# k and q issued ahead of the centroids, other idle products on TensorE, and one placed copy cut in two

## The chip, the core and the metric

The kernel runs on one core of a Trainium2 chip. The core has a matrix engine (TensorE, PE in the profile), a vector engine (VectorE, DVE), an activation engine (ScalarE, ACT), a general engine (GpSimd, POOL) and SyncE (SP), which here only issues DMAs. The engines run their own instruction streams in order and wait for one another through semaphores. The metric is the device time of the program in microseconds, the median of several runs; lower is better.

## What is computed

The reference is clustered attention over 2 batches of 8 heads, sequence 768, head size 64, followed by two dense feed-forward layers. A query sees a key only if both have the same nearest centroid:

```
q_assign = argmax(einsum("bhsd,hcd->bhsc", q_n, c_n)); k_assign likewise     # c_n: centroids / norm
scores = where(q_assign == k_assign, (q @ k.T) / 8, -1e9)
x = softmax(scores) @ v                                                     # then (1536, 512)
h = x @ moe_w_in;  x = max(0.01 * h, h) @ moe_w_out
h = x @ moe2_w_in; out = max(h, 0)**2 @ moe2_w_out
```

## The kernel before

Heads are worked on in pairs (two heads fill 128 partitions); there are eight pairs. Each operand of the score products is held as a high and a low part, which are placed into a tile `hb` of one head (rows 0 to 63 and 64 to 127, four slots of 768 columns). For the first pair the parts are computed straight into `hb` by VectorE, ScalarE and GpSimd; for later pairs they are computed into a tile `spl` and copied into `hb` by DMAs that SP issues (`place`, L482, letters a to d are the four copies of a head; c is the low part of q, into rows 64 to 127 of slot 0). A unit of attention is two tiles of 128 queries: score products S0 and S1 (L521), row maxima R0 and R1 (L543), exponentials X0 and X1 (L553), row sums RE and RC, the scaling N0 and N1 (L570), transposes Ta to Tc (L583), their copies Ha to Hc and La to Lc (L594, L600) and the products with v, Va to Vc (L618). Tile t writes its scores into PSUM bank set t % 2.

The order on all engines in this part of the program is written by hand. The string `RAMP` (L51) lists the operations of the first pair and the start of the second one by one; every engine takes its own operations in that order. After it a repeating table takes over, then the two feed-forward layers with orders of their own.

Ahead of `RAMP` stand the constants and the loads. SP issues the centroids `ct` (L326), then k and q of pair 0 and of pair 1 (`loads_qk`, L323, tile `rqk`), then v. `prep_centroids` (L333) computes the norm of each centroid: a product and a sum on VectorE (L335, L337), a square root on ScalarE (L339), and on VectorE a lower bound, a reciprocal, one correction step, another reciprocal and the scaling of `ct` (L341 to L351). TensorE transposes `ct` into `ctp` (L353), and ScalarE copies that into `cbd` (L355, L356), a block-diagonal tile which GpSimd has set to zero (L170). Products of k and q with `cbd` are the dots (L391) from which VectorE chooses the clusters (L782, L785). ScalarE needs a function table for the square root and another for the exponential, so it runs two table loads. While TensorE has nothing to do it runs idle products of an identity matrix (`warm_up`, L328, nine ahead of `ctp` and three behind it, and `fill`, L772), whose results nobody reads. A float32 product of this kind appears as two records.

`head_0` (L705) makes the parts of head 0: on VectorE four operations (L714, L721, L714, L725) that follow the centroid work in its order, on ScalarE two (L712) that follow the copies of `cbd`.

Of the kernel before, what the change touches and what calls it, by code (L numbers as in the profile page):

```python
# [8 lines left out]
F32 = mybir.dt.float32  # L9
# [5 lines left out]
AF = mybir.ActivationFunctionType  # L15
ALU = mybir.AluOpType
# [87 lines left out]
def attention_moe_moe_kernel(  # L104
# [9 lines left out]
    nc = tc.nc  # L114
    NP, _, _, S = qk.shape
# [9 lines left out]
    HALF = S // 2  # L125
# [24 lines left out]
    const = ast.enter_context(tc.tile_pool(name="const", bufs=1))  # L150
    const.tile([128, 120], F32, name="cpad")

    ident = const.tile([128, 128], F32, name="ident")
    make_identity(nc, ident)
    eps = const.tile([128, 1], F32, name="eps")
    nc.gpsimd.memset(eps, 1e-9)
    msc = const.tile([128, 1], F32, name="msc")
    mbi = const.tile([128, 1], F32, name="mbi")
    nc.gpsimd.memset(msc[0:32], BIG)
# [7 lines left out]
    identb = const.tile([128, 128], BF16, name="identb")  # L167
    nc.gpsimd.tensor_copy(out=identb, in_=ident)
    cbd = const.tile([128, HP, 2 * C], F32, name="cbd")
    nc.gpsimd.memset(cbd, 0.0)  # L170
    desc = const.tile([128, 24, C], F32, name="desc")
    for c in range(C):
        nc.gpsimd.memset(desc[:, :, c], float(2 ** (C + 8 - c)))
# [149 lines left out]
            nc.sync.dma_start(out=rqks[p][:, j], in_=qk[p, j])  # L323

    ct = const.tile([128, D], F32, name="ct")
    nc.sync.dma_start(out=ct, in_=cen)  # L326

    def warm_up(n):  # L328
        w = ps_t.tile([128, 512], F32, tag="T", name="warm")
        for i in range(n):  # L330
            nc.tensor.matmul(out=w[:, 0:128], lhsT=ident, rhs=ident, start=True, stop=True)  # L331

    def prep_centroids():  # L333
        sq = const.tile([128, D], F32, name="sq")
        nc.vector.tensor_tensor(out=sq, in0=ct, in1=ct, op=ALU.mult)  # L335
        ss = const.tile([128, 1], F32, name="ss")
        nc.vector.tensor_reduce(out=ss, in_=sq, axis=AX.X, op=ALU.add)  # L337
        n0 = const.tile([128, 1], F32, name="n0")
        nc.scalar.activation(out=n0, in_=ss, func=AF.Sqrt)  # L339
        nc.scalar.activation(out=const.tile([128, 1], F32, name="tab"), in_=eps, func=AF.Exp)  # L340
        nc.vector.tensor_scalar(out=n0, in0=n0, scalar1=1e-30, scalar2=None, op0=ALU.max)  # L341
        rn = const.tile([128, 1], F32, name="rn")
        nc.vector.reciprocal(out=rn, in_=n0)
        nc.vector.scalar_tensor_tensor(
            out=n0, in0=ss, scalar=rn, in1=n0, op0=ALU.mult, op1=ALU.add
        )
        nc.vector.tensor_scalar(
            out=n0, in0=n0, scalar1=0.5, scalar2=1e-6, op0=ALU.mult, op1=ALU.add
        )
        nc.vector.reciprocal(out=rn, in_=n0)  # L350
        nc.vector.tensor_scalar(out=ct, in0=ct, scalar1=rn, scalar2=None, op0=ALU.mult)  # L351
        ctp = ps_t.tile([128, 512], F32, tag="T", name="ctp")
        nc.tensor.transpose(ctp[0:64, 0:128], ct, ident)  # L353
        cview = ctp[0:64, 0:128].rearrange("p (a h c) -> p a h c", h=2, c=C)
        nc.scalar.copy(out=cbd[0:64, :, 0:C], in_=cview[:, :, 0])  # L355
        nc.scalar.copy(out=cbd[64:128, :, C : 2 * C], in_=cview[:, :, 1])  # L356
# [125 lines left out]
    def place(p, j, which):  # L482

        h = 2 * p + j
        r = slice(64 * j, 64 * j + 64)
        if h not in hbs:
            hbs[h] = heads[h % 3]
        hb = hbs[h].bitcast(F32)
        sp = spl[p].bitcast(F32)
        copies = {  # L490
            "a": (hb[0:64, 0:3], sp[r, 0:3]), "b": (hb[0:64, 3], sp[r, 0]),
            "c": (hb[64:128, 0], sp[r, 3]), "d": (hb[64:128, 1], sp[r, 1]),
        }
        for c in which:
            o, i = copies[c]
            nc.sync.dma_start(out=o, in_=i)
# [196 lines left out]
    for h, j in ((2, 3), (0, 2), (0, 3), (1, 2), (1, 3)):  # L693
        nc.sync.dma_start(
            out=heads[h][80:128, j].bitcast(F32), in_=heads[2][80:128, 2].bitcast(F32)
        )
    warm_up(9)
    prep_centroids()
    eighth = const.tile([128, 1], F32, name="eighth")
    warm_up(3)  # L700

    for h in range(2):
        hbs[h] = heads[h]
# [90 lines left out]
    def mask_mm(h, part, cols=(0, 1, 2)):  # L794
        j, g = 1 - part // 2, part % 2
        mt = mask_t[h, part, cols] = ps_t.tile([128, 512], F32, tag="T", name="ohT")
        for i in cols:
            o = (2 * (g * (KC // 2) + i) + h) * C
            nc.tensor.transpose(
                mt[0:80, i * 128 : (i + 1) * 128], flat[:, 1 - j, o : o + 80], ident  # L800
            )

    def mask_act(h, part, cols=(0, 1, 2), act=None):
        j, g = 1 - part // 2, part % 2
        c = slice(cols[0] * 128, (cols[-1] + 1) * 128)
        mt = mask_t.pop((h, part, cols))[64:80, c]
        o = hbs[h][64:80, 3 - j, g * HALF + c.start : g * HALF + c.stop]
        act = j == 1 if act is None else act
        if j == 1:
            (nc.scalar.copy if act else nc.vector.tensor_copy)(out=o, in_=mt)  # L810
        elif act:
            nc.scalar.activation(
                out=o, in_=mt, func=AF.Identity, bias=mbi[64:80], scale=msc[64:80]
            )
        else:
            nc.vector.tensor_scalar(
                out=o, in0=mt, scalar1=msc[64:80], scalar2=mbi[64:80], op0=ALU.mult, op1=ALU.add
            )
# [20 lines left out]
    for h in range(2):  # L839
        for i in range(4):  # L840
            if (h, i) != (0, 2):
                first_ops[f"mk{h}{i}"] = lambda h=h, i=i: mask_mm(h, i)
                first_ops[f"ma{h}{i}"] = lambda h=h, i=i: mask_act(h, i)
                first_ops[f"ma{h}{i}A"] = lambda h=h, i=i: mask_act(h, i, act=True)
                first_ops[f"ma{h}{i}D"] = lambda h=h, i=i: mask_act(h, i, act=False)
        first_ops[f"ms{h}"] = lambda h=h: place_masks(1, h, (2, 3, 0, 1))
        for c in "abcd":
            first_ops[f"pl{h}{c}"] = lambda h=h, c=c: place(1, h, c)
    first_ops.update(head_1())

# [14 lines left out]
    for g, c in enumerate("abc"):  # L865
# [28 lines left out]
        "oT": oh_trans,  # L894
        "st": mask_rows,
        "pl00": lambda p: place(p, 0, "abcd"),
        "pl01": lambda p: place_masks(p, 0),
        "pl10": lambda p: place(p, 1, "abcd"),
# [11 lines left out]
    for op in RAMP.split():  # L910
        if ":" in op:
            name, i = op.split(":")
            step(name, int(i), unit_ops[name])
        elif "@" in op:
            name, i = op.split("@")
# [6 lines left out]
    for u in range(-1, NU + 5):  # L922
# [9 lines left out]
        for op in PLAN[u % UPP].split():  # L932
            if ":" in op:
                name, lag = op.split(":")
                i = u - int(lag)
                if 0 <= i < NU:
                    step(name, i, unit_ops[name])
            else:
                name, ahead = op.split("@")
# [6 lines left out]
        w = u - (NU - UPP)  # L946
# [610 lines left out]
```

## Time and profile before

| What | us |
|---|---|
| median of 3 runs | 733.88 (733.5 to 734.03) |
| the profiled execution, own time | 734.87 |
| its span, first to last instruction | 733.1 |
| PE / POOL / DVE / ACT busy | 725.6 / 596.5 / 562.3 / 500.0 |

The profiled execution's own time is 1.77 us above its span: what lies around the instructions. It is also 0.99 us above the median of the runs. A row of the trace in order of time reads: start, duration, engine, line, operation, what it writes and reads, size, count, and in brackets how long the engine had been idle and what is taken to have ended that. Where that last part names an engine that had long been done, it was something else that came last, often a DMA.

### The profile page before, as it was taken

Reading aid. Unit: us, or ns where it says so; the run is one execution under the profiler, and the core shown is the slowest. Engines: PE = TensorE matmul, PEld = TensorE weight load, DVE = VectorE, ACT = ScalarE, POOL = GpSimd, SP = SyncE. Lnnn points to the kernel's source line nnn. Section 1 sums busy time; section 2 is a strip of 40 time slices with the busy share of each in tenths; the row PEclk is TensorE's granted clock in tenths of the full one; section 3 lists DMA queues with packets and bytes.
Section 4 is the critical chain, followed back from the end, with each engine's and each line's share of the span. In section 5 each row is a group of like instructions: output and inputs, shape, how many; then the busy total and the mean of one; then the engine's idle time right before and its main releaser. Section 6 shows DMA issues by size and latency. Waiting matters only on the chain.

```text
span 733.1 us, 11920 instructions
## 1 busy us (share of the span) xinstructions
PE 725.6 (99%) x4246; PEld 644.4 (88%) x4246; DVE 562.3 (77%) x893; ACT 500.0 (68%) x923; POOL 596.5 (81%) x562
## 2 busy tenths in 40 slices
PE   9999999999999999999999999999999999999997
PEld 8999999999998888888888888888888898888986
DVE  7989999999998737686776866887677595775946
ACT  7978988988998777447365464658847558375561
POOL 6999999999959977987787877899798786787840
PEclk9999999999999999999999999999999999999999
DMA  5693573662611312212121131111113112121004
GB/s 150 161 219 104 128 172 104 136 167 66 146 54 59 115 58 79 94 58 97 56 79 57 58 115 58 59 58 58 58 59 114 59 58 79 64 89 57 1 1 173
DMA packets 17756, 65.58 MB, mean 89 GB/s; under 512 B 3120, under 2 KB 6320, under 8 KB 12704
## 3 DMA queue, kind: packets, MB, share of 16 engines
q1 hardware_dynamic: 17696, 64.81, 30.0%
q8 instruction: 34, 0.56, 0.3%
q14 instruction: 26, 0.21, 0.1%
HBM read 43.02 MB, written 3.15 MB: 63 GB/s over the span
## 4 chain that ended last, share of the span: by engine, by line
PE 91%; DVE 4%; ACT 2%; POOL 1%; issue 1%; DMA 1%; ACTq 0%; DVEq 0%; POOLq 0%
PE h L1043 33%; PE o L1274 18%; PE h L1274 10%; PE A L618 8%; PE S L521 7%; PE T L583 7%; PE o L1121 4%; PE S L391 2%; DVE nm L543 1%; ACT e L553 1%; DVE el L600 1%; PE warm L331 1%; DMA out<-q 1%; POOL e L570 0%; PE dots L391 0%
## 5 line engine op out<-in xcount | busy, mean ns | idle before, releaser
L1043 PE MATMUL h<-xh,wh 128*128 128x512 f32 x272 | 106.7, 392 | 0.0
L1043 PE MATMUL h<-xh,wl 128*128 128x512 f32 x272 | 106.1, 390 | 0.0
L1043 PE MATMUL h<-xl,wh 128*128 128x512 f32 x272 | 106.1, 390 | 0.0
L1228 POOL TENSOR_TENSOR gl<-t,gh 128x512 fp32r<-128x512 f32 x56 | 79.9, 1444 | 31.9 <-ACT gh L1225 21.9
L197 POOL TENSOR_TENSOR wl<-ws,wh 128x1024 fp32r<-128x1024 f32 x28 | 67.8, 2420 | 41.8 <-ACT wh L194 41.8
L570 POOL TENSOR_SCALAR e<-e,r 128x768 f32<-128x768 f32 x96 | 87.4, 919 | 12.5 <-PE T L583 6.8
L600 DVE TENSOR_TENSOR el<-T,eh 128x512 fp32r<-128x512 f32 x144 | 94.6, 683 | 3.0 <-ACT eh L594 1.9
L543 DVE TENSOR_REDUCE nm<-S 128x1 f32<-128x768 f32 x96 | 90.9, 949 | 3.9 <-PE S L391 2.5
L553 ACT ACTIVATE e<-S,nm 128x768 f32<-128x768 f32 x96 | 87.3, 910 | 9.6 <-DVE nm L543 5.8
L521 PE MATMUL S<-hb 128*128 128x384 f32 (+1 forms) x384 | 89.6, 347 | 1.6 <-ACT eh L594 0.4
L594 ACT CAST eh<-T 128x512 fp32r<-128x512 f32 x144 | 79.7, 590 | 9.6 <-PE T L583 9.4
L1173 DVE TENSOR_TENSOR h<-h,q 128x512 f32<-128x512 f32 x42 | 29.4, 699 | 70.6 <-PE h L1043 45.3
L197 POOL TENSOR_TENSOR wl<-wt,wh 128x1024 fp32r<-128x1024 f32 x31 | 75.5, 2434 | 9.6 <-ACT wh L194 8.7
L618 PE MATMUL A<-eh,vv 128*128 128x256 f32 x288 | 80.2, 307 | 0.0
L583 PE MATMUL T<-ident,e 128*128 128x128 f32 x576 | 79.5, 273 | 0.0
L618 PE MATMUL A<-el,vv 128*128 128x256 f32 x288 | 73.0, 283 | 0.0
L583 PEld LDWEIGHTS T<-ident,e 128*128 128x128 f32 x576 | 68.9, 143 | 3.0
L224 ACT ACTIVATE wt<-wraw 128x1024 f32<-128x1024 f32 (+1 forms) x33 | 36.8, 1115 | 47.5 <-POOL ws L286 47.3
L521 PEld LDWEIGHTS S<-hb 128*128 128x128 f32 (+1 forms) x384 | 62.2, 189 | 3.7 <-ACT e L553 1.9
L1228 DVE TENSOR_TENSOR gl<-h,gh 128x512 fp32r<-128x512 f32 x70 | 48.0, 688 | 18.3 <-ACT h L1210 7.9
L1043 PEld LDWEIGHTS h<-xh,wh 128*128 128x128 f32 x272 | 51.1, 188 | 11.6 <-DVE gl L1228 1.1
L1043 PEld LDWEIGHTS h<-xh,wl 128*128 128x128 f32 x272 | 51.0, 188 | 10.6
(202 smaller groups left out, 2088.3 us busy)
## 6 DMA issues: line engine op xcount, KB each, us to landing
wraw<-w SPq DMA_DIRECT2D x32, 1024.0 KB, 4.7
hb<-spl SPq DMA_DIRECT2D x14, 576.0 KB, 4.7
hb<-spl SPq DMA_DIRECT2D x42, 192.0 KB, 5.1
rqk<-qk SPq DMA_DIRECT2D x16, 384.0 KB, 3.7
rv<-v SPq DMA_DIRECT2D x8, 384.0 KB, 3.4
out<-q SPq DMA_DIRECT2D x11, 256.0 KB, 2.2
hb<-st SPq DMA_DIRECT2D x56, 24.0 KB, 2.1
hb<-hb SPq DMA_DIRECT2D x5, 144.0 KB, 7.0
```

Of the source, the lines that this page charges most:

```text
L197: last_of["wl"] = eng.tensor_tensor(out=wl, in0=t, in1=wh.bitcast(F32), op=ALU.subtract).ins
L521: nc.tensor.matmul(out=s[:, c, 0:HALF], lhsT=hb[0:k, a, i * 128 : (i + 1) * 128], rhs=hb[0:k, b, c * HALF : (c + 1) * HALF], start=(a == 0 ...
L543: last_of["nm", t] = nc.vector.tensor_reduce(out=n, in_=s_t[t][:, :, 0:HALF], axis=AX.XY, op=ALU.max, negate=True).ins
L553: nc.scalar.activation(out=e.rearrange("p (a b) -> p a b", a=2), in_=s_t.pop(t)[:, :, 0:HALF], func=AF.Exp, bias=n_t.pop(t), scale=1.0, ac ...
L570: last_of["norm"] = nc.gpsimd.tensor_scalar(out=e_t[t], in0=e_t[t], scalar1=r_t[t // 2][:, t % 2 : t % 2 + 1], scalar2=1.0, op0=ALU.mult, ...
L583: nc.tensor.transpose(T[:, o : o + 128], e_t[2 * u + b][:, kc * 128 : (kc + 1) * 128], ident)
L594: last_of["eh", u, g] = nc.scalar.copy(out=eh[:, 2 * g : 2 * g + 2, :].rearrange("p a b -> p (a b)"), in_=T_t[u, g]).ins
L600: last_of["el"] = last_of["el", u, g] = nc.vector.tensor_tensor(out=el[:, 2 * g : 2 * g + 2, :].rearrange("p a b -> p (a b)"), in0=T_t.pop ...
L618: nc.tensor.matmul(out=A, lhsT=w, rhs=m[:, kc, :], start=(kc == 0 and i == 0), stop=(kc == KC - 1 and i == 1),)
L1043: nc.tensor.matmul(out=out, lhsT=l, rhs=r, start=(first and i == 0), stop=(i == n - 1), skip_group_check=not first,)
L1228: eng.tensor_tensor(out=lo[n], in0=full[n], in1=hi[n].bitcast(F32), op=ALU.subtract)
L1274: nc.tensor.matmul(out=out, lhsT=l, rhs=r, start=(fresh and i == 0), stop=(stop and i == 2), skip_group_check=True,)
```

## The change

The changed kernel sends `ct` from ScalarE's queue and leaves SP to begin with k and q. The square root gets a bias of 1e-30 from a new tile `tiny` (set by GpSimd), and the lower bound on VectorE is dropped. `cbd` is set to zero by VectorE. `warm_up` takes a list of operands: two float32 products of the zeroed `cbd`, five of `ident` and three of the bfloat16 `identb` ahead of `ctp`, six of `identb` behind it. In `RAMP` the copy c of the first head of pair 1 is replaced by two copies of half its columns: e stands ahead of `ql1` and `ms0`, f where c stood.

```
@@ RAMP @@
-        "R0:4 S1:4 st@1 ql0@1 N1:2 RE:3 pl0d Vb:1 Lc:1 X0:4 ql1@1 Ta:2 R1:4 ms0 Vc:1 Ha:2 Tb:2 RC:3 "
-        "FC:1 La:2 Tc:2 Hb:2 S0:5 FA:1 Hc:2 Lb:2 N0:3 X1:4 Va:2 Lc:2 Vb:2 pl0c N1:3 scale@2 khi@2 "
+        "R0:4 S1:4 st@1 ql0@1 N1:2 RE:3 pl0d Vb:1 Lc:1 X0:4 pl0e ql1@1 Ta:2 R1:4 ms0 Vc:1 Ha:2 Tb:2 RC:3 "
+        "FC:1 La:2 Tc:2 Hb:2 S0:5 FA:1 Hc:2 Lb:2 N0:3 X1:4 Va:2 Lc:2 Vb:2 pl0f N1:3 scale@2 khi@2 "
@@
+    tiny = const.tile([128, 1], F32, name="tiny")
+    nc.gpsimd.memset(tiny, 1e-30)
@@
-    nc.gpsimd.memset(cbd, 0.0)
+    nc.vector.memset(cbd, 0.0)
+    flat_cbd = cbd.rearrange("p h c -> p (h c)")
@@
-    nc.sync.dma_start(out=ct, in_=cen)
-
-    def warm_up(n):
+    nc.scalar.dma_start(out=ct, in_=cen)
+
+    def warm_up(*todo):
         w = ps_t.tile([128, 512], F32, tag="T", name="warm")
-        for i in range(n):
-            nc.tensor.matmul(out=w[:, 0:128], lhsT=ident, rhs=ident, start=True, stop=True)
+        for x, n in todo:
+            for i in range(n):
+                nc.tensor.matmul(out=w[:, 0:128], lhsT=x, rhs=x, start=True, stop=True)
@@ prep_centroids @@
-        nc.scalar.activation(out=n0, in_=ss, func=AF.Sqrt)
+        nc.scalar.activation(out=n0, in_=ss, func=AF.Sqrt, bias=tiny)
         nc.scalar.activation(out=const.tile([128, 1], F32, name="tab"), in_=eps, func=AF.Exp)
-        nc.vector.tensor_scalar(out=n0, in0=n0, scalar1=1e-30, scalar2=None, op0=ALU.max)
@@ place @@
+            "e": (hb[64:128, 0, 0:HALF], sp[r, 3, 0:HALF]),
+            "f": (hb[64:128, 0, HALF:S], sp[r, 3, HALF:S]),
@@
-    warm_up(9)
+    warm_up((flat_cbd, 2), (ident, 5), (identb, 3))
     prep_centroids()
     eighth = const.tile([128, 1], F32, name="eighth")
-    warm_up(3)
+    warm_up((identb, 6))
```

ScalarE's order at the program's start, before. A wait in brackets is for the engine named (DMAHW: a DMA); `n` holds the norm, `ss` the sum of squares, `tab` a value that nobody reads.

```order
L1553 UNCONDITIONAL_BRANCH [waits barrier_Pool_Activation_PE_DVE_SP_release]
L339 ACT_TABLE_LOAD
L339 ACTIVATE n_193<-ss 128x1 [waits DVE_49]
L340 ACT_TABLE_LOAD
L340 ACTIVATE tab<-eps 128x1 [waits Pool_49]
L355 COPY cbd<-ctp 64x4x16 [waits PE_49,Pool_49]
```

The same place in the changed kernel:

```order
L329 DMA ct<-cen 128x64
L343 ACT_TABLE_LOAD [waits DVE_49]
L343 ACTIVATE n_196<-ss,tiny 128x1 [waits Pool_49]
L344 ACT_TABLE_LOAD
L344 ACTIVATE tab<-eps 128x1
L358 COPY cbd<-ctp 64x4x16 [waits PE_49]
```

The issue of `ct` now stands first. The square root has two waits, for VectorE's sum and for GpSimd's `tiny`, and the one for VectorE stands ahead of the table load.

SP's order where pair 1 is placed, before: the copies b and d, the four mask copies from `st`, then c, then the next head's.

```order
L496 DMA hb<-spl 64x768 [waits DMAHW0_49]
L503 DMA hb<-st 16x384 [waits DMAHW1_49,Activation_49]
L503 DMA hb<-st 16x384 [waits DMAHW4_49]
L496 DMA hb<-spl 64x768 [waits DMAHW5_49,Pool_49]
L496 DMA hb<-spl 64x2304 [waits DMAHW6_49,PE_49]
```

The same place in the changed kernel:

```order
L501 DMA hb<-spl 64x768 [waits DMAHW0_49]
L501 DMA hb<-spl 64x384 [waits DMAHW1_49,Pool_49]
L508 DMA hb<-st 16x384 [waits DMAHW2_49,Activation_49]
L508 DMA hb<-st 16x384 [waits DMAHW5_49]
L501 DMA hb<-spl 64x384 [waits DMAHW6_49,Pool_49]
L501 DMA hb<-spl 64x2304 [waits DMAHW7_49,PE_49]
```

Half of the copy has moved ahead of the mask copies, and the other half stands where the whole stood.

## Rows read from the trace of the kernel before

**Rows 1.** The page, part 4: shares of the chain that ended last.

```profile
PE 91%; DVE 4%; ACT 2%; POOL 1%; issue 1%; DMA 1%; ACTq 0%; DVEq 0%; POOLq 0%
```

**Rows 2.** Busy time by stage: stretch, its length, each engine's busy us, clock, DMA.

```profile
34.00:49.00 15.00, 13.75 (x105) 12.89 (x103) 12.29 (x25) 10.89 (x25) 13.52 (x14) 1.00 0.89 226
60.00:200.00 140.00, 140.00 (x1101) 137.29 (x1100) 132.36 (x243) 123.41 (x277) 135.04 (x161) 1.00 0.55 130
```

**Rows 3.** VectorE in order of time, first 9 us.

```profile
2.42 0.23 DVE L335 TENSOR_TENSOR sq<-ct 128x64 f32<-128x64 f32 x1 [2.42 <-DMA ct<-cen]
...
3.17 0.15 DVE L341 TENSOR_SCALAR n<-n 128x1 f32<-128x1 f32 x1 [0.27 <-ACT n L339]
3.36 0.16 DVE L343 RECIPROCAL rn<-n 128x1 f32<-128x1 f32 x1
...
4.20 0.26 DVE L351 TENSOR_SCALAR ct<-ct,rn 128x64 f32<-128x64 f32 x1
5.18 0.55 DVE L714 TENSOR_SCALAR hb<-rqk 64x768 fp32r<-64x768 f32 x1 [0.73 <-DMA rqk<-qk]
...
8.21 0.36 DVE L782 TENSOR_REDUCE m<-dots 128x12 f32<-128x192 f32 x1
```

**Rows 4.** The chain of waits, first 15 us: start, us, what.

```profile
1.41 4.21 PE warm L331 x18
...
6.88 1.26 PE dots L391 x12
...
12.51 1.46 DVE hb L816 x3
```

**Rows 5.** ScalarE in order of time, first 9 us.

```profile
0.73 1.28 ACT L339 ACT_TABLE_LOAD   x1 [0.73 <-PEq L1547]
2.94 0.20 ACT L339 ACTIVATE n<-ss 128x1 f32<-128x1 f32 x1 [0.92 <-DVE ss L337]
3.16 1.28 ACT L340 ACT_TABLE_LOAD   x1
...
5.93 0.21 ACT L355 COPY cbd<-ctp 64x64 f32<-64x64 f32 x1 [1.28 <-PE ctp L353]
```

**Rows 6.** ScalarE's line L564, an activation with a bias from a tile: ns min/median/max.

```profile
L564 ACT ACTIVATE r<-r,eps x6: 298/298/300, 16.9 to 37.2; 128x2 f32<-128x2 f32 x6
```

**Rows 7.** SP's issues in order of time, first 20 us.

```profile
0.74 0.38 SPq L326 DMA_DIRECT2D ct<-cen  x1
1.17 1.84 SPq L323 DMA_DIRECT2D rqk<-qk  x4
```

**Rows 8.** DMA issues of the first 6 us: KB each, median us to landing.

```profile
ct<-cen SPq DMA_DIRECT2D x1, 32.0 KB, 1.7
```

**Rows 9.** The tile rqk, first 40 us: its six loads.

```profile
DMA to landing us min/median/max: 4.0/4.7/5.7
```

**Rows 10.** The chain of waits, 30 to 60 us: bfloat16 products.

```profile
53.48 0.18 PE ohT L473 x3
```

**Rows 11.** TensorE in order of time, 34 to 42 us.

```profile
34.44 1.04 PE L583 MATMUL T<-ident,e 128*128 128x128 f32 x8
35.84 0.58 PE L521 MATMUL S<-hb 128*128 128x384 f32 x2 [0.36 <-ACT q L645]
```

**Rows 12.** ScalarE in order of time, 34 to 42 us.

```profile
35.26 0.37 ACT L645 COPY q<-A 64x256 f32<-64x256 f32 x1
```

**Rows 13.** SP's issues, 29 to 36 us.

```profile
29.31 3.28 SPq L503 DMA_DIRECT2D hb<-st  x4
32.68 4.21 SPq L496 DMA_DIRECT2D hb<-spl  x4
```

**Rows 14.** DMA issues from 32.6 to 33.45 us.

```profile
hb<-spl SPq DMA_DIRECT2D x1, 192.0 KB, 2.9
```

**Rows 15.** GpSimd in order of time, 27 to 36 us.

```profile
27.76 1.01 POOL L373 TENSOR_TENSOR spl<-rqk,spl 128x384 fp32r<-128x384 f32 x1
29.63 1.03 POOL L373 TENSOR_TENSOR spl<-rqk,spl 128x384 fp32r<-128x384 f32 x1
```

More of the change, by code (lines that the diff above doesn't have):

```diff
@@ L846, in attention_moe_moe_kernel @@
         first_ops[f"ms{h}"] = lambda h=h: place_masks(1, h, (2, 3, 0, 1))
-        for c in "abcd":
+        for c in "abcdef":
             first_ops[f"pl{h}{c}"] = lambda h=h, c=c: place(1, h, c)
```

## The prediction

> **What bounds the kernel now.** I read the shares of the chain first: TensorE makes 91% of it [rows 1]. Then the stages: from 60 to 200 us TensorE is busy 140.00 of 140.00 us, while from 34 to 49 us it is busy 13.75 of 15.00 [rows 2]. So once the program is past about 50 us, time is TensorE's work and nothing else, and whatever the start gains or loses reaches the end one for one. The change touches nothing behind 45 us, so I need two things: when the start hands over, and the gaps of the second pair's first products.
>
> At the start the chain of waits shows TensorE without a gap from 1.41 us on, but what it runs are idle products: 18 records in 4.21 us, then the dots from 6.88 us [rows 4]. They fill time and are not what is waited for. The work that cannot come earlier is VectorE's: it waits for the centroids until 2.42, has them scaled at 4.20 + 0.26 = 4.46, stands idle 0.73 us until k has landed, begins the parts of head 0 at 5.18 and the choice of clusters at 8.21 [rows 3]; the chain itself passes to VectorE at 12.51 [rows 4]. So today k's landing sets the start, and the centroid work is finished 0.7 us ahead of it.
>
> **The loads.** k's issue moves from 1.17 to 0.74, the place that the centroids leave [rows 7]. k takes 4.0 us from issue to landing [rows 9], so it lands at 4.74 instead of 5.17: 0.43 us to be had, if VectorE is free by then.
>
> The centroids go out on ScalarE, which is free at 0.73, as SP is at 0.74 [rows 5, 7]. Alone they took 1.7 us and VectorE began at 2.42 [rows 8, 3]. Now they travel at the same time as k, and the trace has no DMA from ScalarE, so I bound it: 2.42 if nothing changes, 4.74 if they finish only with k. Nothing in the rows lets them come sooner, since their issue starts no earlier. I take 2.9: they are 32 KB, which is near to their own row, but twelve times as much k now shares the engines with them.
>
> The Trainium skill speaks against this edit (DMA: Bandwidth & Descriptors, "Issuing engines are not separate DMA queues"): DMAs of SP and ScalarE end up on the same 16 engines and interleave, and a second issuing engine saves only the issue time. No row here shows it; by it the centroids lose their lead over k, and the sum moves towards the rival that I price below with the landing of k.
>
> **The square root.** The lower bound falls away: 3.36 - 3.17 = 0.19 us of VectorE's chain [rows 3]. The bias comes from a tile, and such an activation takes 298 ns where this one takes 0.20 us: 0.10 us more [rows 6, 5]. The large term is the table load. Today it runs from 0.73 to 2.01, before the sum of squares exists, and costs nothing [rows 5]. In the changed order the wait for that sum stands ahead of the load, because the activation now has two waits. So the load's 1.28 us falls between the sum and the root. Net: 1.28 + 0.10 - 0.19 = +1.19 us. From the centroids' arrival to the scaled centroids it was 4.46 - 2.42 = 2.04 us and becomes 3.23 us.
>
> Queued behind this on VectorE are the parts of head 0, which need only k and q. They begin at 2.9 + 3.23 + 0.02 = 6.15 instead of 5.18: +0.97 us, with 2.42 at the low end +0.49 us, with 4.74 at the high end +2.8 us. The 0.43 us of k's earlier landing is lost, because k now waits for VectorE. On ScalarE the second table load and `tab` follow and end at about 2.9 + 0.52 + 1.28 + 0.30 + 1.28 + 0.20 = 6.5; the copies of `cbd` came at 5.93 behind `ctp` [rows 5] and come some 0.95 later, about 6.9, so that load stays covered. Behind those copies ScalarE's parts of head 0, and GpSimd, which waits for them, shift by the same. I see no work on these engines that would close up again before TensorE takes over, so I carry +0.97.
>
> **The idle products.** Seven float32 products are 14 records at 4.21 / 18 = 0.234 us, 3.3 us; three bfloat16 ones cost 0.18 / 3 = 0.06 each at the upper level [rows 4, 10], 0.4 together at the lower. They start when VectorE has zeroed `cbd`, about 1.0 us, and end at about 4.7. The zeroing itself lies in VectorE's wait of 2.42 us. Today the queue of idle products holds `ctp` back and then the dots; in the change it holds nothing back, since the scaled centroids come at 6.13. TensorE instead stands still from 4.7 to 6.1. The dots begin at about 7.4 and at 1.26 us [rows 4] the dots of k are done at 8.7, before VectorE is ready at 8.21 + 0.97 = 9.18. So 0.5 us of cover is there, as long as TensorE runs at the upper level.
>
> **The copy in two parts.** S0 of the second pair's first tile begins at 35.84 after 0.36 us of idle; the transposes before it end at 34.44 + 1.04 = 35.48 [rows 11]. The bracket names a copy of ScalarE that ends at 35.63 [rows 12], but S0 doesn't wait for that one in the program; it waits for an earlier exponential and for the placed copies. Copy c is issued at 32.68 and takes 2.9 us [rows 13, 14]: it lands at 35.58. That is the wait. In the change half e needs only the first half of the low part, ready at 27.76 + 1.01 = 28.77 [rows 15], and goes out then; f is needed three tiles later. Next in line is the end of the transposes at 35.48, so 0.36 us go. The cost is on SP: the mask copies behind e, issued from 29.31 on [rows 13], start about 0.1 us late and carry half a copy more ahead of them; the last issue ends at 32.59, 2.9 us ahead of S0, which covers it. With that cover gone the gain would shrink to nothing, so this term lies between 0 and -0.36. I take -0.36: the two rows agree within 0.1 us.
>
> **Sum.** +0.97 - 0.36 = +0.61 us on the profiled execution's own time of 734.87, that is 735.48. The median of the runs is 0.99 lower, and the same sum there gives 733.88 + 0.61 = 734.5. The terms' ends (+0.49 and -0.36; the centroids at 3.4, halfway into k, +1.45 and -0.36) give 734.0 to 735.0.
>
> **The rivals.**
> The clock of TensorE (slower). Idle products take 0.234 us a record up to 5.6 us; dots of the same pass take 1.26 / 12 = 0.105 [rows 4]: the first run at the lower of the two levels (1.2 and 2.4 GHz), the others at the upper, and the rise came after some 5 us of unbroken products. In the change the products break off for about 1.4 us just there. If the rise comes after the dots have begun, the 24 dots and the idle products between cost up to 2 x 1.26 + about 1 = 3.5 us more, of which 0.5 is covered: up to +3 us. Against it: a short pause need not undo anything, and products do start 0.4 us sooner. With the level rising around 10 us it is about +1.2, 735.7; from about 10 us on it decides over slower. Range 734.9 to 737.
> The centroids land only with k: +2.8 - 0.36 = +2.4, 736.3.
> The split copy frees nothing, because the bracket is right and ScalarE ends the wait: 733.88 + 0.97 = 734.85.
> The table load doesn't bite: then VectorE has the centroids at 2.9 + 1.95 = 4.85, 0.32 sooner than it begins head 0 now, and the sum is -0.32 - 0.36 = -0.68, 733.2. Against it stands the order of ScalarE.
>
> **How the numbers follow.** The forecast 0.48; the clock 0.26; no gain from the copy 0.12; the load doesn't bite 0.10; centroids with k 0.04. A measurement of this kernel can tell about 0.2%, 1.5 us, from no change: below 732.4 or above 735.4. Faster needs the last rival and more, 0.05. Slower is 0.15 of the clock's share, 0.04 of the centroids with k and 0.04 of late centroids elsewhere, 0.23. The rest, 0.72, is no change. The range reaches from 733.2, where the load doesn't bite, to 736.1; it leaves out half of that rival (0.05) and the upper third of the clock's share with the late centroids (0.12).
>
> **What would show it.** A table load directly ahead of the square root, with VectorE idle over 1.2 us in front of its reciprocal; head 0's first part at about 6.1 with no wait for k; a gap on TensorE from 4.7 to 6.1; the dots' duration (1.26 us for twelve, or twice that) for the clock; no idle time ahead of the second pair's first S0. I am wrong if VectorE begins head 0 at 4.8, or if the shift of about 1 us at 8 us is gone by 50 us.

## The result and the profile after

| What | before | after |
|---|---|---|
| median, us | 733.88 (733.31 to 735.07, 5 runs) | 740.79 (740.52 to 741.37, 5 runs) |
| the profiled execution, own time / span | 734.87 / 733.1 | 740.74 / 739.0 |

The change makes the kernel slower by 6.9 us: the ratio is 1.009, with a 95% interval from 1.0079 to 1.0101. The prediction was 734.5, its range ended at 736.1. It was wrong.

The shares of the chain after the change, beside [rows 1], and two stretches shifted by 7 us against those of [rows 2]:

```profile
PE 91%; ACT 3%; DVE 3%; DMA 1%; issue 1%; POOL 0%; SPq 0%; ACTq 0%
```

```profile
41.00:56.00 15.00, 14.00 (x105) 13.20 (x105) 12.42 (x24) 11.09 (x26) 13.67 (x15) 1.00 0.85 215
67.00:207.00 140.00, 140.00 (x1104) 137.15 (x1103) 132.35 (x242) 123.34 (x278) 134.96 (x162) 1.00 0.55 130
```

The later stage is the same as before, 140.00 of 140.00 us on TensorE. So the loss lies ahead of it. The chain of waits of that stretch (start, us, what), to be held against [rows 4]:

```profile
0.73 3.46 DMA ct<-cen
...
4.78 1.28 ACT L343
...
8.62 2.64 PE dots L394 x12
...
12.27 2.40 PE dots L394 x12
...
19.35 0.41 DVE hb L821
```

The two loads of ScalarE's table that ran at 0.73 and 3.16 [rows 5] now run at 4.78 and 6.39. The mask copies of VectorE (`hb`) began at 12.51 in the kernel before and begin at 19.35 now: +6.84 us, which is the size of the whole loss. It has two parts. Up to the dots of k the chain runs through the centroids' load and the table load, which TensorE's queue has to wait for. From there to 19.35 it is TensorE's own queue, and everything in it takes about twice as long: twelve dots 2.64 us where it was 1.26.

VectorE after the change, in order of time, beside [rows 3]:

```profile
4.22 0.23 DVE L339 TENSOR_TENSOR sq<-ct 128x64 f32<-128x64 f32 x1 [3.22 <-DMA ct<-cen]
...
6.41 0.16 DVE L346 RECIPROCAL rn<-n 128x1 f32<-128x1 f32 x1 [1.71 <-ACT n L343]
...
7.25 0.25 DVE L354 TENSOR_SCALAR ct<-ct,rn 128x64 f32<-128x64 f32 x1
7.42 0.55 DVE L719 TENSOR_SCALAR hb<-rqk 64x768 fp32r<-64x768 f32 x1
...
11.29 0.36 DVE L787 TENSOR_REDUCE m<-dots 128x12 f32<-128x192 f32 x1 [0.89 <-PE dots L394]
```

The centroids are there 1.80 us later (4.22 against 2.42). The reciprocal waits 1.71 us for the root. Head 0 begins 2.24 us later and without a wait for k, and the first choice of clusters 3.08 us later, because it now waits for the dots.

TensorE after the change, in order of time:

```profile
1.05 1.22 PE L335 MATMUL warm<-cbd 128*128 128x128 f32 x4 [1.05 <-DVE cbd L172]
2.06 2.34 PE L335 MATMUL warm<-ident 128*128 128x128 f32 x10
4.20 0.53 PE L335 MATMUL warm<-identb 128*128 128x128 bf16 x3
7.56 0.42 PE L356 MATMUL ctp<-ident,ct 128*64 128x128 f32 x1 [2.83 <-DVE ct L354]
```

It stands still from 4.73 to 7.56 us. The trace's records of the granted clock begin with the upper level (2.4 GHz) at 6.5 us in the kernel before and at 19.9 us in the changed one. Where no record stands, the column for the clock shows 1.00, so ahead of that the level has to be read from durations, as with the dots above.

The loads: of SP's issues the first now holds k, and the centroids' row of the DMA issues answers to [rows 8]:

```profile
0.73 1.81 SPq L326 DMA_DIRECT2D rqk<-qk  x4
...
ct<-cen ACTq DMA_DIRECT2D x1, 32.0 KB, 3.5
```

3.5 us to landing, against 1.7. The Trainium skill (DMA: Bandwidth & Descriptors, "Issuing engines are not separate DMA queues") says that such transfers interleave on the same 16 engines whichever engine issued them, and that the second issuer saves only the issue. The trace agrees, with this 3.5.

### The profile page after: what moved, and what is told of

It is laid out like the page before. It is cut to its first block, busy times and chain, and to the rows that moved or that the text cites. A ratio compares the mean times of both kernels' runs of the same rounds, so it can differ in the third digit from the quotient of the medians.

```text
span 739.0 us, 11920 instructions
## 1 busy us (share of the span) xinstructions
PE 729.6 (99%) x4245; PEld 648.2 (88%) x4245; DVE 562.1 (76%) x893; ACT 499.2 (68%) x923; POOL 595.8 (81%) x562
## 4 chain that ended last, share of the span: by engine, by line
PE 91%; ACT 3%; DVE 3%; DMA 1%; issue 1%; POOL 0%; SPq 0%; ACTq 0%
PE h L1048 33%; PE o L1279 19%; PE h L1279 10%; PE A L623 8%; PE S L526 7%; PE T L588 7%; PE o L1126 4%; ACT e L558 2%; PE S L394 2%; DVE nm L548 1%; DVE el L605 1%; PE dots L394 1%; ACT eh L599 1%; DMA ct<-cen 0%; PE dots L779 0%
## 5 line engine op out<-in xcount | busy, mean ns | idle before, releaser
L558 ACT ACTIVATE e<-S,nm 128x768 f32<-128x768 f32 x96 | 87.2, 909 | 10.3 <-DVE nm L548 6.1
```

The lines of the kernel that those rows point to most:

```text
L558: nc.scalar.activation(out=e.rearrange("p (a b) -> p a b", a=2), in_=s_t.pop(t)[:, :, 0:HALF], func=AF.Exp, bias=n_t.pop(t), scale=1.0, ac ...
```

## The experiments

Each time stands beside runs of the kernel before on the same chip (medians 734.17 to 734.42). "Upper level from" is the start of the first clock record at that level.

| Run | changed against | median, us | ratio (95%) | TensorE idle ahead of `ctp` | upper level from |
|---|---|---|---|---|---|
| no_pause | after | 735.33 | 1.0015 (1.0006 to 1.0024) | 0.80 | 5.5 |
| ct_first | after | 738.60 | 1.0057 (1.0042 to 1.0072) | 1.11 | 16.3 |
| no_bias | after | 738.84 | 1.0063 (1.0046 to 1.0081) | 1.65 | 5.3, fell at 8.7, again 15.6 |
| before_pause | before | 739.99 | 1.0083 (1.0064 to 1.0101) | 1.18 | 16.6 |
| both_undone | after | 734.66 | 1.0017 (1.0001 to 1.0033) | none | 5.7, fell at 19.3, again 26.1 |
| np_ct_first | after | 734.85 | 1.0011 (1.0002 to 1.0020) | 0.83 | 3.9 |
| split_only | before | 734.56 | 1.0003 (0.9994 to 1.0011) | none | 7.6 |
| swap | after | 738.44 | 1.0048 (1.0034 to 1.0062) | 1.14 | 17.3 |
| weak_fill | after | 738.01 | 1.0040 (1.0024 to 1.0056) | 0.70 | 6.5, fell at 9.9, again 16.7 |
| np_no_bias | after | 734.01 | 1.0002 (0.9994 to 1.0011) | none | 7.1, fell at 10.5, again 13.9 |
| undone_fill | after | 733.71 | 1.0005 (0.9988 to 1.0023) | none | 17.3 |
| undone_f32 | after | 732.95 | 0.9978 (0.9965 to 0.9990) | none | 4.6 |
| before_weak | before | 733.25 | 0.9993 (0.9984 to 1.0001) | none | 7.2 |

The clock column is that of the one profiled execution, which need not be the median one.

### Is it the pause on TensorE?

no_pause fills the pause of the changed kernel and leaves both delays of the centroids as they are:

```diff
-    warm_up((flat_cbd, 2), (ident, 5), (identb, 3))
+    warm_up((flat_cbd, 2), (ident, 5), (identb, 3), (ident, 7))
```

> The changed kernel with seven more float32 identity products ahead of the transpose of the centroids, so that TensorE has no pause between 4.7 and 7.5 us; nothing else differs. Theory P (the pause keeps TensorE at its lower level until 19.9 us): dots at the upper level, twelve in 1.3 us instead of 2.64, VectorE's first choice of clusters 0.9 us sooner, the first mask copy at about 15.5 instead of 19.35, time 740.8 - 3.8 = 737.0. Theory L (only the late centroids cost, the level matters little): 740.8 or a little more.

before_pause opens a pause in the kernel before and changes nothing else:

```diff
-    warm_up(9)
+    warm_up(4)
```

> The kernel before with four idle products ahead of the transpose instead of nine: all of them float32 identity products, centroids and k on time, but a pause on TensorE from 3.3 to 4.6 us. Theory P: the rise comes late and the time is 733.9 + 2 to 4 = 736 to 738. Theory K (the kind of product): no change, 733.9; without late centroids it can even be 0.3 lower, as the dots start sooner.

TensorE of no_pause, in order of time:

```profile
4.52 2.28 PE L335 MATMUL warm<-ident 128*128 128x128 f32 x14
7.60 0.30 PE L356 MATMUL ctp<-ident,ct 128*64 128x128 f32 x1 [0.80 <-DVE ct L354]
...
8.41 1.52 PE L394 MATMUL dots<-cbd,rqk 128*128 128x32 f32 x12 [0.18 <-ACT cbd L359]
```

VectorE of no_pause at the mask copies:

```profile
14.55 1.46 DVE L821 TENSOR_SCALAR hb<-ohT,msc,mbi 16x128 fp32r<-16x128 f32 x3 [0.46 <-PE ohT L804]
```

TensorE of before_pause, in order of time:

```profile
1.41 2.07 PE L331 MATMUL warm<-ident 128*128 128x128 f32 x8 [1.41 <-POOL ident masks.py:199]
4.66 0.42 PE L353 MATMUL ctp<-ident,ct 128*64 128x128 f32 x1 [1.18 <-DVE ct L351]
...
6.16 2.61 PE L391 MATMUL dots<-cbd,rqk 128*128 128x32 f32 x12
```

The two runs are mirror images. In no_pause the dots begin at 8.41, nearly where they begin in the changed kernel (8.49), and run at the upper level, in 1.52 us. The ratio falls from 1.009 to 1.0015, so about 0.0075 x 734 = 5.5 us of the loss go with the pause. The mask copies begin at 14.55 instead of 19.35, although head 0 begins no sooner (7.46): 4.80 us of the 6.84 are the lower level's. Both go further than theory P had said (masks at 15.5 us, a time of 737.0). In before_pause the dots begin at 6.16, sooner than the 6.72 of the kernel before in the same view (6.88 in the chain of [rows 4]), without any of the changed loads, and run at the lower level, and the kernel is 0.0083 x 734 = 6.1 us slower, where 2 to 4 were expected. A loss that needs late centroids is refuted by the second run, and a loss that is only the centroids' delay itself by the first. But no_pause adds float32 products as well as filling a gap; weak_fill, below, asks whether any products do.

### How large is each delay of the centroids?

ct_first takes the centroids back to SP's queue ahead of k; no_bias takes the bias away and the lower bound back:

```diff
-    nc.scalar.dma_start(out=ct, in_=cen)
+    nc.sync.dma_start(out=ct, in_=cen)          # ct_first
```

```diff
-        nc.scalar.activation(out=n0, in_=ss, func=AF.Sqrt, bias=tiny)
+        nc.scalar.activation(out=n0, in_=ss, func=AF.Sqrt)      # no_bias
+        (after tab) nc.vector.tensor_scalar(out=n0, in0=n0, scalar1=1e-30, scalar2=None, op0=ALU.max)
```

> The changed kernel with the centroids sent by SP ahead of k and q again. Centroids at 2.42 instead of 4.22, scaled at about 5.7, so head 0 begins 1.7 us sooner and the pause on TensorE is 1.0 us instead of 2.8. Theory P in its weak form (a pause of 1.0 us does nothing): 740.8 - 1.7 - 3.8 = 735.3. Theory P in its strong form (any pause at that place delays the rise) or theory K (zero and bfloat16 products do not bring the rise): 739.1.

> The changed kernel with the square root without a bias and the lower bound on VectorE back: the table load stands ahead of the wait again. All theories: load at the program's start, head 0 begins at 6.3 instead of 7.42, pause on TensorE 1.6 us. 739.6 if the level still rises late, 735.8 if a pause of 1.6 us does not hold it back.

VectorE of ct_first and TensorE of ct_first:

```profile
2.50 0.23 DVE L339 TENSOR_TENSOR sq<-ct 128x64 f32<-128x64 f32 x1 [1.50 <-DMA ct<-cen]
...
5.69 0.55 DVE L719 TENSOR_SCALAR hb<-rqk 64x768 fp32r<-64x768 f32 x1
```

```profile
6.76 2.77 PE L394 MATMUL dots<-cbd,rqk 128*128 128x32 f32 x12
```

Each delay by itself leaves a pause, 1.11 and 1.65 us, and with it two thirds of the loss. The time of ct_first, 738.60, is near the 739.1 that two theories gave: that any pause at that place delays the rise, or that the zero and bfloat16 products don't bring it. The second can't be the whole cause, since before_pause has float32 products alone. That of no_bias, 738.84, lies between its two cases. In no_bias the level is up when the dots of k run (1.52 us) and falls right behind them. The clock by stretches in no_bias (stretch, length, TensorE busy, clock):

```profile
5.00:8.00 3.00, 1.45 (x15) 1.00 0.99 340
9.00:15.00 6.00, 6.00 (x29) 0.50 0.43 68
```

From 5 to 8 us, ahead of the fall, TensorE was busy 1.45 of 3 us; then it works 6 us on end at half the clock.

np_ct_first and np_no_bias are the same two kernels with two and four more float32 idle products, `(ident, 2)` and `(ident, 4)`, so that each delay stands with less of its pause (0.83 us in np_ct_first) or none (np_no_bias):

> The changed kernel with the centroids back on SyncE ahead of k, and two more float32 idle products so that TensorE does not stand still while the table load holds the centroids up. What stays against the kernel before is the table load behind the wait. Theory: with the clock in order the table load costs only what it moves VectorE: head 0 begins at about 5.7 us against 5.18, the first choice of clusters 0.5 later, and the shift at the second pair is 0.3 to 0.6 us: time 734.4 to 735.2, between before (734.4) and the run with the late centroids and no pause (735.3). Rival, the table load itself (ScalarE held up) costs more than its place on VectorE's path: 736 or more, with ScalarE as the engine that is waited for between 6 and 12 us.

> The changed kernel without the bias (table load early, lower bound on VectorE back) and with four more float32 idle products: of the two delays only the late landing of the centroids is left, with TensorE kept busy. Theory: the centroids land with k at about 4.2, head 0 begins at 6.2 us against 7.4 in the run with both delays and 5.6 with the table load alone; the clock rises before the dots; time 734.6 to 735.4. Rival (the late landing is no delay by itself, only the table load is): head 0 begins at 5.2 or earlier, time 734.2 or less.

Head 0 begins at 5.60 and 6.19 us in them, as expected, and the times are 1.0011 and 1.0002 of before; the second, 734.01, is below the 734.6 to 735.4 expected. By the intervals the table load costs 0.1 to 1.5 us, the late landing -0.4 to 0.8, and both together 0.4 to 1.8 (no_pause). These are costs against the kernel before, so the rest of the change, which can gain time by itself (undone_f32, below), is in them. They are less than what VectorE moves by: head 0 begins 1.0 us later in np_no_bias than in [rows 3]. Where that goes, the traces show. TensorE of np_ct_first:

```profile
10.93 1.15 PE L804 MATMUL ohT<-ident,pads 128*80 128x128 f32 x9 [0.19 <-DVE pads L790]
```

In np_ct_first and in no_pause TensorE waits 0.19 us for VectorE's choice ahead of the transposes of the masks, so there VectorE sets the masks. Head 0 is 0.42 us late in np_ct_first (5.60) and the masks 0.19 (12.70); in no_pause it is 2.28 late (7.46) and the masks 2.04 (14.55). Both say that head 0 can begin as late as 5.4 us before the masks move. By this, the late landing alone would move the masks by about 0.8 us (an estimate: 6.19 - 5.4), and the second pair gives 0.2 us of the shift back in both traces.

The profile of np_no_bias itself cannot show that, and it goes against the pause as the only condition. It is of the slowest of the ten executions (736.49). The clock by stretches:

```profile
1.05:7.00 5.95, 5.95 (x31) 1.00 0.85 274
7.00:10.50 3.50, 3.50 (x33) 1.00 1.05 254
10.50:13.90 3.40, 3.40 (x16) 0.50 0.33 64
```

TensorE works from 1.05 us on without a gap, and the level, which came up at 7.1, still falls at 10.5. Why is open.

### Which queue makes the centroids late?

swap exchanges the two loads: the centroids first on SP, k at the same moment on ScalarE, and no bias.

```diff
-            nc.sync.dma_start(out=rqks[p][:, j], in_=qk[p, j])
+            (nc.scalar if p == 0 and j == 1 else nc.sync).dma_start(out=rqks[p][:, j], in_=qk[p, j])
```

> As both_undone, but k of pair 0 goes out on ScalarE's queue at the same time as the centroids on SyncE's, instead of 0.43 us behind them: the two queues of the change with their loads exchanged. Theory S (two loads that go out together share the 16 engines, whichever queue holds which): the centroids land at 3.5 to 4.2 us, VectorE's first product of them begins after 3.5, head 0 at 5.5 to 6.2, time 734.5 to 736 with little pause on TensorE and up to 739 with a pause above 1 us. Theory Q (ScalarE's queue is slow to start): the centroids land at 2.4, k at 4.7 to 5.2, head 0 begins at 4.8 to 5.2, the time is 733.4 to 734.4, at or just below before.

VectorE of swap:

```profile
3.77 0.23 DVE L339 TENSOR_TENSOR sq<-ct 128x64 f32<-128x64 f32 x1 [2.78 <-DMA ct<-cen]
```

3.77 us, where the centroids issued 0.43 us ahead of k arrive at 2.4 to 2.6. So going out together with k delays them on either queue (3.0 us to landing on SP's, 3.5 on ScalarE's); which queue holds them matters less. The time of 738.44 comes again with a pause, of 1.14 us.

### Does the copy in two parts keep its gain?

split_only is the kernel before with e and f in `RAMP` and in `place`, as in the change.

> The kernel before with only the copy c of the second pair's first head cut into the halves e and f. Theory G (given back): S0 of the second pair's first tile begins about 0.36 us earlier than in the kernel before, S1 begins at the same time as before, since the exponential of the tile two back ends at the same time; the shift from S1 on is 0 and the time is no different (733.9 to 734.8, ratio 1.000 within 0.001). Rival, the prediction's own step: 0.36 us is kept to the end (ratio 0.9995, the trace shows -0.3 at S1 and after). Rival, the additional DMA ahead of the mask copies delays them: S0 no earlier, S1 later, ratio above 1.0005.

TensorE of split_only and ScalarE of split_only at the second pair's first products, and S1 in the kernel before:

```profile
34.93 1.04 PE L585 MATMUL T<-ident,e 128*128 128x128 f32 x8
35.76 0.61 PE L523 MATMUL S<-hb 128*128 128x384 f32 x2
...
37.66 0.62 PE L523 MATMUL S<-hb 128*128 128x384 f32 x2
```

```profile
37.40 0.20 ACT L555 ACTIVATION_READ_ACCUMULATOR e<-S,nm 128x1 f32 x1
```

```profile
37.42 0.59 PE L521 MATMUL S<-hb 128*128 128x384 f32 x2
```

S0 no longer waits: the transposes ahead of it stand 0.49 us behind the kernel before (34.93 against 34.44; the clock rose later in this execution), S0 stands 0.08 ahead of it (35.76 against 35.84), so 0.57 us have gone. But S1 (37.66) follows the end of the exponential at 37.60, which reads the scores of the tile two back out of the same PSUM bank set, and it stands 0.24 behind (37.42) again. Of 0.57 us, 0.25 are kept against this execution of the kernel before. That lies between the two theories, and the time, 1.0003, cannot tell 0.25 us. The changed kernel shows the same pattern; TensorE, beside [rows 11]:

```profile
41.36 1.04 PE L588 MATMUL T<-ident,e 128*128 128x128 f32 x8
42.19 0.61 PE L526 MATMUL S<-hb 128*128 128x384 f32 x2
...
44.09 0.62 PE L526 MATMUL S<-hb 128*128 128x384 f32 x2
```

It is 6.92 us behind the kernel before at the transposes, 6.35 at S0 and 6.67 at S1. The wait itself is not the same in every execution: without the split, the same S0 lost another 0.6 us in before_pause and gained 0.4 in before_weak, so the landing of copy c moves by half a microsecond or more. TensorE of before_weak, whose copy c is whole:

```profile
34.58 1.04 PE L584 MATMUL T<-ident,e 128*128 128x128 f32 x8
...
37.32 0.62 PE L522 MATMUL S<-hb 128*128 128x384 f32 x2
```

From the start of the transposes to S1 are 2.74 us here, 2.73 in split_only and in the changed kernel, 2.98 in the kernel before and 3.62 in before_pause. So the split gains nothing against one execution of the whole copy, 0.25 against another and 0.9 against a third.

### What is left with both delays undone, and does the kind of product count?

both_undone joins ct_first and no_bias; the idle products of the change and the copy in two parts stay.

> The changed kernel with the centroids back on SyncE ahead of k, and the square root without its bias (the lower bound on VectorE is back, so the table load should stand early again). The three bfloat16 and seven float32 idle products, the zeroed cbd on VectorE and the copy in two parts stay. Theory: the loss is the sum of two delays of the centroids' chain and of the pause on TensorE that they open. Then the scaled centroids come at about 4.5 us, no pause stands ahead of the transposition (products end at 4.7), VectorE begins head 0 at about 5.2, the dots run at 0.105 us a record, and the time is 733.5 to 734.9, no different from before. Rival 1, the weaker idle products keep the clock low by themselves: dots of k take 2.6 us, the time is 739 or more. Rival 2, the second pair's copy in two parts costs something: no pause, but 1 to 2 us above before, with the shift arising at about 35 to 45 us.

Its ten times go from 732.89 to 738.5. ScalarE and TensorE in its profiled execution, of 737.34 us, and the clock behind that:

```profile
13.38 0.83 ACT L384 CAST vv<-rv 128x768 fp32r<-128x768 f32 x1 [1.74 <-DMA rv<-v]
```

```profile
16.88 1.86 PE L527 MATMUL S<-hb 128*128 128x384 f32 x8 [1.58 <-ACT e L559]
```

```profile
20.00:26.00 6.00, 6.00 (x27) 0.50 0.54 189
```

In this execution v lands only at 13.4 us, 10.3 after its issue; in undone_f32, with the same issue at 3.06, it takes 8.0 and ScalarE comes to it at 11.56 without a wait. Here ScalarE waits 1.74 us, the exponential behind it is late, TensorE stands still for 1.58 us, and the clock falls at 19.3. The median lies in the expected range, the spread does not. undone_fill puts idle products into that place:

```diff
-"S1:0 R0:0 A5 lok mk13 R1:0 d1c X0:0 d1d ma13 X1:0 vlo@0 S0:1 ma12 ..."
+"S1:0 R0:0 A5 lok mk13 R1:0 d1c X0:0 d1d ma13 X1:0 vlo@0 W3 S0:1 ma12 ..."      # W3: fill(4)
```

> The run with both delays undone (centroids first on SyncE, no bias), with four more float32 idle products (8 records, 0.9 us) ahead of S0 of the first pair's tile 1, where TensorE stood still from 15.3 to 16.9 us in its profile and the clock fell at 19.3. Theory: that second pause is what spread that kernel's times from 732.9 to 738.5; filled by half or more, no time is above 735.5, the median 733.2 to 734.2 (ratio 0.9985 to 1.0000), the clock does not fall between 6 and 700 us. Rival (the fall at 19 us has nothing to do with the pause): the times spread to 737 and more as before, the clock falls again in some executions, median 734.5 to 735.5.

Nine of its 12 executions lie between 732.53 and 734.15, three between 737.8 and 739.2. The profile is of one of the three, and its clock rises only at 17.3 although TensorE had no pause. So the second pause is not the whole cause of the spread. weak_fill asks whether bfloat16 products count as much as float32 ones: they fill the pause of the changed kernel.

```diff
-    warm_up((flat_cbd, 2), (ident, 5), (identb, 3))
+    warm_up((flat_cbd, 2), (ident, 5), (identb, 27))
```

> The changed kernel with 27 bfloat16 idle products ahead of the centroids instead of three, so that TensorE's stand-still is filled with the weakest products at hand and not with float32 ones. At 0.18 us each at the lower level (0.53 for three) the added 24 take up to 4.2 us, 1.5 at the upper level. Theory P (the stand-still alone keeps the clock low, the kind does not matter): the clock has risen when the dots begin, dots of k take 1.3 to 1.6 us, time 735 to 736.5, as in the run with seven more float32 products (735.3). Rival K (bfloat16 products do not count enough): dots of k take 2.6 to 2.8 us, the rise comes after 15 us, time 738.5 to 741.

TensorE of weak_fill, and its clock:

```profile
4.20 2.76 PE L335 MATMUL warm<-identb 128*128 128x128 bf16 x27
7.66 0.30 PE L356 MATMUL ctp<-ident,ct 128*64 128x128 f32 x1 [0.70 <-DVE ct L354]
```

```profile
10.00:16.00 6.00, 6.00 (x28) 0.50 0.29 45
```

The pause left is 0.70 us, no longer than the 0.80 of no_pause. Yet the clock, which rose at 6.5, falls again at 9.9, and three of four times lie at 738, one at 735.27; the ten of no_pause end at 736.53. Neither case came whole: the dots of k take 1.52 us, as theory P said, and the time is near the rival's 738.5. In these four executions the kind counts, so filling the pause is not enough by itself; it was float32 products that undid the loss. The last two runs test it where no pause is.

```diff
-    warm_up((flat_cbd, 2), (ident, 5), (identb, 3))     # undone_f32: undone_fill with
+    warm_up((flat_cbd, 2), (ident, 7))
-    warm_up((identb, 6))
+    warm_up((ident, 3))
```

```diff
-    warm_up(9)                                          # before_weak: the kernel before with
+    warm_up(4); warm_up(17, identb)
```

> The run with both delays undone and the additional idle products ahead of tile 1, but with every idle product in float32: two of cbd and seven of ident ahead of the transposition of the centroids (ending at about 5.2 us), three of ident behind it. In the run that it is compared with, 3 of 12 executions lay at 737.8 to 739.2 and its profile showed TensorE without a pause and yet at the lower level until 17 us. Theory K2 (the kind of idle product weighs too: weak ones leave the rise to chance even without a pause): with float32 alone no execution is above 735.5, the rise comes before 7 us, the median is 733.0 to 733.8 and the ratio 0.998 to 0.9995. Rival P (only pauses matter; those three executions had another cause, the earlier start of the products): again about one execution in four at 737 or more. Rival, no gain: the v load holds ScalarE at 13 us and the median is 734.0 to 734.6.

> The kernel before with five of its nine float32 idle products ahead of the transposition replaced by 17 bfloat16 ones, which fill about the same time (3.5 to 5.3 us), so no pause is opened; nothing else is changed. Theory K2 (the kind weighs): some or most executions rise late, at 737.5 to 740, the median or at least the highest of them above 737, while no execution of the kernel before was above 735.7. Rival P (only the pause matters): all executions between 733.3 and 735.5, ratio 1.000 within 0.001.

TensorE and VectorE of undone_f32, in order of time:

```profile
2.07 2.92 PE L335 MATMUL warm<-ident 128*128 128x128 f32 x14
4.82 0.27 PE L357 MATMUL ctp<-ident,ct 128*64 128x128 f32 x1
...
5.61 1.52 PE L395 MATMUL dots<-cbd,rqk 128*128 128x32 f32 x12
```

```profile
4.46 0.55 DVE L720 TENSOR_SCALAR hb<-rqk 64x768 fp32r<-64x768 f32 x1
...
7.48 0.36 DVE L788 TENSOR_REDUCE m<-dots 128x12 f32<-128x192 f32 x1
```

undone_f32 takes 732.95 us, 0.22% below before (0.10 to 0.35%; 0.18% by the medians), and its 11 times end at 734.16, below the 735.5 of theory K2. It beats both kernels. before_weak goes against the same theory: 17 bfloat16 products between float32 ones, with no pause, and no late execution among 11 (732.79 to 734.5). So weak products did harm in weak_fill, where they carry 2.8 us next to a pause, and none was seen where 1.8 us of them stand between float32 products. Whether they, or chance, made the three late executions of undone_fill stays open: the kernel before itself had three of 21 at 737.4 to 737.8 in this last series, and none in those ahead of it.

Why undone_f32 gains is in the chain of the kernel before, in the part that I had not weighed:

```profile
5.84 1.04 PE warm L331 x6
...
8.67 1.26 PE dots L391 x12
...
12.33 0.15 PE ohT L799
```

From the idle products to 12.48 it is TensorE without a break. What sets the masks in the kernel before is TensorE's queue, as long as head 0 begins by about 5.4, and its part that counts begins with the dots: at 6.72 in order of time before, at 5.61 in undone_f32. There the idle products start at 1.05 and let the centroids through 0.6 us sooner (4.82 against 5.42), and the level, up from 4.6 instead of 6.5, shortens the idle products behind them. The masks follow 0.95 us ahead (11.56 against 12.51). The idle products ahead of tile 1 take 0.4 of that back, another 0.25 come at the second pair's S1, and 0.4 between 60 and 700 us; the medians differ by 1.3. The last 0.4 need not be the edit's: held against the same trace, TensorE gains 0.2 us in that stretch in before_weak too and 0.3 in split_only, which change nothing there.

## Why the prediction was wrong

**One for one: right.** The loss of 6.84 us at the masks is still 6.67 us at the second pair, and the medians differ by 6.9. In the two profiles TensorE's shift falls from 6.65 at 60 us to 6.23 at its last product, of which before_weak and split_only show 0.2 to 0.3 without any edit there. (The two profiled executions differ by 5.9; that of before was 0.99 above its median.)

**The idle products as mere filling: wrong for the kernel before.** "They fill time and are not what is waited for" holds for the ones of 1.41 to 5.4 us only if TensorE's queue behind them has room. The same chain [rows 4] shows that it has none up to 12.48. Behind a late VectorE the sentence holds: in no_pause the dots of k end at 9.93 and VectorE is done with head 0 at 10.44, the 0.5 us of cover that were forecast. So the cover was right at the upper level; what the sum left out is that the masks move only when head 0 begins behind about 5.4 us.

**k's landing: a row of one execution.** The wait of 0.73 us for k [rows 3] is in the one profiled execution; in before_pause, split_only, undone_f32 and before_weak, with the same order of loads, head 0 begins at 4.46 to 4.54 without a wait. The 0.43 us "to be had" were hardly there, and the step that dropped them was right for another reason.

**The centroids: mis-sized.** The bounds of 2.42 and 4.74 held; I took 2.9 "near to their own row", and 4.22 was measured, at the end that I priced at 0.04. Two loads that leave together landed within half a microsecond, here (3.3 us for k, 3.5 for the centroids) and in swap (3.5 and 3.0). The rule of the Trainium skill that I set beside it pointed there.

**The table load: right.** From the centroids' arrival to the scaled centroids 3.28 us were measured (7.50 - 4.22) and 3.23 predicted, and the load stands where the order showed it. The root with its bias took 0.29 us, as [rows 6] had it.

**The clock: the step that failed.** The forecast let the dots run at 1.26 us behind a pause. The rival was the right mechanism, with 0.26, and its price was too low twice. It counted the dots and "about 1" for the idle products, "up to +3 us", but every record of TensorE's queue to 19.35 ran at the lower level, the transposes of the masks too. And its likeliest value rested on a rise at about 10 us, for which no row spoke; it came at 19.9. At the masks 4.80 us of the 6.84 are the clock's (19.35 - 14.55, against no_pause), and 2.04 are what the late VectorE leaves; by the times, filling the pause gave 5.5 back. The levels had been read rightly, but from unlike rows: idle products of 128 columns against dots of 32. Like for like, an idle product falls from 0.234 us to 0.13 (four in 0.53 us behind the dots).

**The copy: the right wait, sized from one execution.** The wait was for the copy and not for ScalarE, and it went; against that execution 0.25 us are kept, 0.36 were predicted. I asked what was late next at S0, and not at S1, two rows further on, where the exponential takes 0.3 us back. That c's landing moves from one execution to the next was not in the term: against before_weak nothing is kept.

**The sum: rivals that are not alternatives.** Late centroids, table load and clock were priced each by itself. They come one behind the other: each of the first two opens a pause by itself (1.65 and 1.11 us), together they make it 2.83, and with each of these pauses the level came up late or fell again. A case with all three was not among mine; the shifts measured, 2.04 us from VectorE and 4.80 from the clock, put it at 733.9 + 6.8 = 740.7.

## What to carry to other kernels

Where an edit opens a stand-still on TensorE ahead of its first work, price the whole queue behind it at the lower clock level until a row shows otherwise, or fill the stand-still with float32 products, as no_pause did. Count rivals that feed one another as one case. Where a stall is taken away, look at the next wait of the same engine and the one after it, and take a landing time from more than one execution.

## What was not expected of the hardware

The pause need not stand at the start: 1.58 us without work at 15.3 us were followed by a fall of the level from 19.3 to 26.1 us. A level that had risen in a pause fell again behind it, from 8.7 to 15.6 us in no_bias, with TensorE busy throughout. It fell in np_no_bias too, from 10.5 to 13.9 us, with no gap on TensorE since 1.05. And in one place bfloat16 products did not do what float32 ones did: with 27 of them ahead of a pause of 0.70 us the level was low from 9.9 to 16.7 us in the profiled execution and three of four times were near 738, while no_pause stayed below 736.6 in ten; before_weak shows no such harm.
